# Filling the block-diagonal packed keys of an attention and SwiGLU chain: eight quarter copies and subtractions, or one masked multiplication and a split

## The chip, the cores and the metric

The kernel runs on one core of a Trainium2 chip. The metric is the device time of one execution in microseconds (us), as the median of several executions. TensorE (PE) does the matmuls, VectorE (DVE), ScalarE (ACT) and GpSimd (POOL) the elementwise work, and SyncE (SP) issues most transfers. PEld in the profile is TensorE's weight load.

## The reference, cut to what matters

```python
def sm_attn(qq, kk, vv):
    s = scale * np.matmul(qq, kk.transpose(0, 1, 3, 2))
    s = s - np.max(s, axis=-1, keepdims=True)
    a = np.exp(s)
    a = a / (np.sum(a, axis=-1, keepdims=True) + 1e-09)
    return np.matmul(a, vv)

p_packed = sm_attn(p, k, v)               # 32 packed rows per head
out = sm_attn(q, p_packed, p_packed)      # 576 rows per head, over the 32
x = out rearranged to (4608, 512)
h = x @ w_in; x = (h / (1 + np.exp(-h))) @ w_out
y = (((x @ w1) * (x @ w2)) @ w3) @ w_out2
```

q, k and v are (8, 8, 576, 64): batch, head, row, head dimension. All of it is float32.

## The kernel before, in words

**Precision.** Most float32 products are done as three matmuls (`mm3`, L97): each operand is split into a rounded high part and the low rest (`split`, L93; its copy is recorded as L82 on ScalarE or L86 on VectorE, its subtraction as L91 on VectorE or GpSimd). The three matmuls are recorded as L98, L99 and L100. The first two batches work "plain", with one float32 matmul and no split (L294).

**The main loop** (L1278) runs over 256 items (batch, half of the rows, block of 128 of the 2048 hidden columns). For each item `emit_h` (L826) does six matmuls into `ps_h`, `emit_g` (L839) makes the tanh on ScalarE (`sg`, L841), the product on VectorE (`gg`, L846) and its split into `gh` (ScalarE) and `gl` (GpSimd), and `emit_x2` (L853) does twelve matmuls for the item three places earlier. `ps_h` has two buffers. Weights `mq` of the first product are fetched by `fetch` (L782) and split by VectorE (a cast, L86) and GpSimd (L91). At the end of a half, VectorE and ScalarE move the sums out (`xs`, L883).

**Beside the items** run streams of steps with their own pace (L1087 to L1110): attention for later batches (`Pack` and `Spread`), the weights of the packed rows (`PackIn`), and the decoding of later weights. After item 255 comes a second stage (from L1315), in which nothing of this change runs.

**The part in question.** `Pack` makes the packed rows of four heads at a time (a batch has two such groups, `hg` 0 and 1). After its last product ScalarE scales the result into `pk` (L464), VectorE transposes it into `pkT` (128 x 64: four heads by 32 rows, two halves of the head dimension; L469), and `fill_blocks` (L247, called in L470) writes it into the diagonal blocks of `sbd`, a tile of 128 rows by 2 (high, low) x 2 x 128. The rest of that tile is zero: `blocks` (L221) sets it to zero on GpSimd when it is first made (four tiles, made once plain and once split: eight times). Four quarters of 32 rows are copied one by one, on ScalarE when plain (4 fills) and on VectorE when split (12 fills, batches 2 to 7); when split, four subtractions on VectorE follow for the low parts. `Spread` (L566, L567) later uses `sbd` as the weights of the scores of q (`ps_s`). After the fill, `Pack.tail` (L473) writes the packed rows into `mbd` on VectorE (L490, L492).

**Order of the work.** The instructions of an engine run in the order in which the framework has put them when the program is built, by their place in the program, what they depend on, and a simulated timeline (L1655). The steps of the first 70 us are written out in a list (L70).

`work` (L244) is a pool of three buffers, used for `e1`, `s2` and `sT`.

Of the kernel before, what the change touches and what calls it, by code (L numbers as in the profile page):

```python
# [9 lines left out]
F32 = mybir.dt.float32  # L10
F32R = mybir.dt.float32r
# [4 lines left out]
ALU = mybir.AluOpType  # L16
# [7 lines left out]
def attention_swiglu_chain(  # L24
# [54 lines left out]
    V, A, T, G, DMA = nc.vector, nc.scalar, nc.tensor, nc.gpsimd, nc.sync  # L79
# [4 lines left out]
    def split_hi(hi, src, on_vector=False):  # L84
        if on_vector:
            V.tensor_copy(out=hi, in_=src)  # L86
        else:
            act_copy(hi, src)

    def split_lo(lo, src, hi, eng=None):  # L90
        (eng or V).tensor_tensor(out=lo, in0=src, in1=hi.bitcast(F32), op=ALU.subtract)  # L91

    def split(hi, lo, src, on_vector=False, eng=None):  # L93
        split_hi(hi, src, on_vector)
        split_lo(lo, src, hi, eng)
# [40 lines left out]
    dram = ctx.enter_context(tc.tile_pool(name="dram", bufs=1, space=bass.MemoryType.DRAM))  # L136
    const = ctx.enter_context(tc.tile_pool(name="const", bufs=1))
    ident = const.tile([128, 128], F32, name="ident")

    wi_d = dram.tile([4, DM, 512], F32, name="wi_d")  # L140
    w12_d = dram.tile([128, KM2 // 2, 2, 7, 2, 2, 128], F32, name="w12_d")
# [7 lines left out]
    at = attn.enter_context(tc.tile_pool(name="at", bufs=1, side="right"))  # L149
# [71 lines left out]
    def blocks(name, shape, plain):  # L221

        if zeroed.get(name, (None, None))[0] != plain:
            t = at.tile(shape, F32 if plain else F32R, tag=name, name=name)
            G.memset(t if plain else t.bitcast(F32), 0.0)
            zeroed[name] = plain, t
        return zeroed[name][1]

    def q_blocks(i, plain):
        return blocks(f"sbd{i}", [128, 2, 2, 128], plain)  # L230

    def m_blocks(plain):
        return blocks("mbd", [128, 2, CD, 2, 2, 32], plain)
# [10 lines left out]
    def work(shape, name):  # L244
        return at.tile(shape, F32, tag="work", name=name, bufs=3)

    def fill_blocks(dst, src, plain):  # L247

        quads = [slice(32 * h, 32 * h + 32) for h in range(4)]
        for r in quads:  # L250
            (act_copy if plain else V.tensor_copy)(dst[r, 0, :, r], src[r])
        for r in () if plain else quads:
            V.tensor_tensor(
                out=dst[r, 1, :, r], in0=src[r], in1=dst[r, 0, :, r].bitcast(F32), op=ALU.subtract
            )

    acc = {}

# [100 lines left out]
    class Pack(Rows):  # L359
# [58 lines left out]
        def steps(self):  # L418
# [49 lines left out]
            pkT = at.tile([128, 2, 32], F32, tag="pkT", name="pkT", bufs=2)  # L468
            V.transpose(out=pkT, in_=self.pk[:, 0].rearrange("p (e i) -> p e i", e=2))  # L469
            fill_blocks(q_blocks(2 * (b % 2) + hg, self.lane.plain), pkT, self.lane.plain)  # L470
            yield

# [77 lines left out]
    class Spread(Rows):  # L550
# [11 lines left out]
        def steps(self):  # L562
            b, hg, hv = self.b, self.hg, self.halves
            if b not in a2:
                a2[b] = a2_p.tile([128, 2, 2, S], F32R, tag="a2", name="a2")
            qb = q_blocks(2 * (b % 2) + hg, self.lane.plain)  # L566
            sc = self.scores([qb[:, x] for x in range(2)])  # L567
            n = HB * len(hv)
# [50 lines left out]
        units[-1].tail()  # L619

    make_identity(nc, ident)
    for i in range(2):
        q_blocks(i, True)
    m_blocks(True)

    left = ctx.enter_context(ExitStack())
# [472 lines left out]
    for b in range(2, B - 2, 2):  # L1099
        n, at0 = b + 2, b * H2  # L1100
# [558 lines left out]
```

## Time and profile before

| | us |
|---|---|
| median of 3 executions (1412.35 to 1413.73) | 1413.46 |
| the profiled execution | 1412.14 |
| its span (first to last instruction) | 1410.3 |
| TensorE busy in it | 1362.6 |
| VectorE busy | 1007.0 |
| GpSimd busy | 904.7 |
| ScalarE busy | 732.7 |

The page gives busy time by engine, 40 slices of the span, the chain of work that ended last, and the costliest groups. An instruction's duration in the trace includes time in which it stood blocked after its start, so the same form can be long or short. Idle time before an instruction is put down to what ended it.

### The profile page before, as it was taken

What the parts mean: (1) busy time and instruction counts of PE and PEld (TensorE: products, weight loads), DVE (VectorE), ACT (ScalarE), POOL (GpSimd) and SP (SyncE); (2) the same over time, 40 slices, a digit from 0 to 9 for tenths busy, and PEclk for the clock granted to TensorE, in tenths of its full rate; (3) what the DMA queues carried; (4) which work ended last, traced back from release to release, by engine and by line L of the source; (5) the groups of instructions that cost most, each with busy time, mean ns of one, the idle gap of its engine ahead of it and who ended that gap; (6) DMA issues with size and microseconds to landing.
All of it is one profiled execution on the core that took longest, in us unless ns stands there. A gap on an engine that the chain in (4) does not pass through costs nothing. (4 is left out here: it accounts for less than half of the span.)

```text
span 1410.3 us, 26742 instructions
## 1 busy us (share of the span) xinstructions
PE 1362.6 (97%) x9197; PEld 1313.7 (93%) x9197; DVE 1007.0 (71%) x1760; ACT 732.7 (52%) x1641; POOL 904.7 (64%) x855
## 2 busy tenths in 40 slices
PE   7799899999999999999999999999999999999998
PEld 5488799999899998999999999899999999999998
DVE  5887857668877569887769756776675766656755
ACT  6866555655666565575455644543344343433432
POOL 2778855865779766789577553756574755737632
PEclk9899999999999999999999999999999999999999
DMA  8688544754667535685457648756667676566751
GB/s 311 202 285 284 161 150 136 226 161 135 199 195 223 168 121 143 197 256 155 135 172 242 213 138 280 231 167 207 209 173 218 206 210 209 170 215 206 214 164 53
DMA packets 191558, 272.95 MB, mean 194 GB/s; under 512 B 18752, under 2 KB 112320, under 8 KB 191424
## 3 DMA queue, kind: packets, MB, share of 16 engines
q1 hardware_dynamic: 173168, 251.20, 57.9%
q10 hardware_dynamic: 18256, 20.06, 4.1%
q8 instruction: 73, 1.20, 0.4%
q14 instruction: 61, 0.50, 0.1%
HBM read 209.06 MB, written 62.13 MB: 192 GB/s over the span
## 5 line engine op out<-in xcount | busy, mean ns | idle before, releaser
L98 PE MATMUL ps_x<-gh,wo 128*128 128x288 f32 x1024 | 301.3, 297 | 3.7 <-DVE xs L883 2.4
L99 PE MATMUL ps_x<-gh,wo 128*128 128x288 f32 x1024 | 300.6, 296 | 0.0
L91 POOL TENSOR_TENSOR gl<-gg,gh 128x288 fp32r<-128x288 f32 x256 | 229.5, 899 | 99.3 <-ACT gh L82 77.6
L100 PE MATMUL ps_x<-gl,wo 128*128 128x288 f32 x1024 | 290.3, 297 | 2.0 <-POOL gl L91 1.7
L1481 DVE TENSOR_TENSOR o<-o,ps_o 128x768 f32<-128x768 f32 x137 | 130.1, 952 | 103.3 <-PE ps_o L1499 102.5
L98 PEld LDWEIGHTS ps_x<-gh,wo 128*128 128x128 f32 x1024 | 192.2, 188 | 7.0 <-DVE xs L883 3.2
L91 POOL TENSOR_TENSOR mq<-mr,mq 128x256 fp32r<-128x256 f32 x168 | 140.6, 837 | 90.1 <-DVE mq L86 43.4
L99 PEld LDWEIGHTS ps_x<-gh,wo 128*128 128x128 f32 x1024 | 192.6, 188 | 2.0 <-issue 1.2
L100 PEld LDWEIGHTS ps_x<-gl,wo 128*128 128x128 f32 x1024 | 188.3, 188 | 5.0 <-POOL gl L91 4.1
L846 DVE SCALAR_TENSOR_TENSOR gg<-sg,ps_h 128x288 f32<-128x288 f32 x256 | 114.7, 448 | 107.1 <-ACT sg L841 68.6
L82 ACT ACTIVATE gh<-gg 128x288 fp32r<-128x288 f32 x256 | 112.7, 442 | 149.4 <-DVE gg L846 137.7
L98 PE MATMUL ps_h<-a,mq 128*128 128x288 f32 x512 | 156.2, 305 | 17.6 <-DVE gg L846 13.2
L99 PE MATMUL ps_h<-a,mq 128*128 128x288 f32 x512 | 152.3, 297 | 0.0
L100 PE MATMUL ps_h<-a,mq 128*128 128x288 f32 x512 | 151.9, 297 | 0.0
L91 POOL TENSOR_TENSOR lfa<-y,lfa 128x384 fp32r<-128x384 f32 x69 | 78.7, 1141 | 104.5 <-ACT lfa L82 92.2
L841 ACT ACTIVATE sg<-ps_h 128x288 f32<-128x288 f32 x256 | 103.2, 405 | 79.8 <-PE ps_h L100 50.7
L98 PEld LDWEIGHTS ps_h<-a,mq 128*128 128x128 f32 x512 | 96.8, 189 | 26.6 <-DVE gg L846 19.4
L1499 PE MATMUL ps_o<-w,lfs 128*128 128x256 f32 x828 | 119.3, 282 | 1.9 <-DVE o L1481 1.5
L1341 PE MATMUL ps_a<-xct,ws 128*128 128x384 f32 x576 | 116.3, 335 | 0.4 <-ACT p L82 0.4
L1499 PEld LDWEIGHTS ps_o<-w,lfs 128*128 128x128 f32 x828 | 112.3, 189 | 2.7 <-DVE o L1481 1.8
L1341 PEld LDWEIGHTS ps_a<-xct,ws 128*128 128x128 f32 x576 | 100.1, 188 | 0.7 <-ACT p L82 0.7
L99 PEld LDWEIGHTS ps_h<-a,mq 128*128 128x128 f32 x512 | 96.9, 189 | 2.7 <-issue 1.0
(217 smaller groups left out, 3297.5 us busy)
## 6 DMA issues: line engine op xcount, KB each, us to landing
ws<-w_d SPq DMA_DIRECT2D x192, 256.0 KB, 3.0
wa<-w_d SPq DMA_DIRECT2D x144, 256.0 KB, 3.1
mr<-m_d SPq DMA_DIRECT2D x144, 128.0 KB, 2.5
raw<-in_moe_w_dram SPq DMA_DIRECT2D x32, 512.0 KB, 4.3
w_d<-w12s ACTq DMA_DIRECT2D x56, 256.0 KB, 2.7
wz<-wi_d SPq DMA_DIRECT2D x48, 256.0 KB, 3.9
m_d<-ms SPq DMA_DIRECT2D x96, 128.0 KB, 3.0
x_d<-xs SPq DMA_DIRECT2D x20, 576.0 KB, 3.4
```

The source lines that it names most:

```text
L82: return A.activation(out=dst, in_=src, func=ACTF.Copy, scale=mul)
L91: (eng or V).tensor_tensor(out=lo, in0=src, in1=hi.bitcast(F32), op=ALU.subtract)
L98: T.matmul(out=dst, lhsT=wh, rhs=xh, start=start, stop=False)
L99: T.matmul(out=dst, lhsT=wl, rhs=xh, start=False, stop=False)
L100: return T.matmul(out=dst, lhsT=wh, rhs=xl, start=False, stop=stop)
L841: ins = A.activation(out=sg, in_=ps, func=ACTF.Tanh, scale=0.5)
L846: ins = V.scalar_tensor_tensor(out=gg, in0=sg, scalar=1.0, in1=ps, op0=ALU.add, op1=ALU.mult)
L1341: ins = T.matmul(out=bank, lhsT=w[:, kt, wp], rhs=xt[:, kt, xp], start=first and (kt, n) == (0, 0), stop=last and (kt, n) == (1, 2), skip_ ...
L1481: V.tensor_tensor(out=oacc[k], in0=oacc[k], in1=ps, op=ALU.add)
L1499: T.matmul(out=ps[:, t], lhsT=l[:, lp], rhs=w[:, wp], start=fresh and t != 1 and n == 0, stop=done and t != 0 and n == 2, skip_group_check ...
```

## The change

A constant `mask` of 128 x 4 has a one where row / 32 equals the column. `fill_blocks` multiplies `pkT`, spread over four heads, by the mask, spread over the 32 rows, on VectorE in one instruction that writes the whole 128 x 256 block, zeros included. When plain, it writes `sbd` directly. When split, it writes a `work` buffer, ScalarE copies the high part out of it, and GpSimd subtracts for the low part. The zeroing of `sbd` goes; five small memsets for the mask come at the start. `m_blocks` stays as it was.

```diff
+    mask = const.tile([128, 4], F32, name="mask")
...
+    sbd = {}
+
     def q_blocks(i, plain):
-        return blocks(f"sbd{i}", [128, 2, 2, 128], plain)
+
+        if sbd.get(i, (None, None))[0] != plain:
+            sbd[i] = plain, at.tile([128, 2, 2, 128], F32 if plain else F32R, tag=f"sbd{i}", name=f"sbd{i}")
+        return sbd[i][1]
...
     def fill_blocks(dst, src, plain):
 
-        quads = [slice(32 * h, 32 * h + 32) for h in range(4)]
-        for r in quads:
-            (act_copy if plain else V.tensor_copy)(dst[r, 0, :, r], src[r])
-        for r in () if plain else quads:
-            V.tensor_tensor(
-                out=dst[r, 1, :, r], in0=src[r], in1=dst[r, 0, :, r].bitcast(F32), op=ALU.subtract
-            )
+        wide = [128, 2, 4, 32]
+        whole = dst[:, 0] if plain else work([128, 2, 128], "blk")
+        V.tensor_tensor(
+            out=whole.rearrange("p e (h n) -> p e h n", h=4), in0=src.unsqueeze(2).to_broadcast(wide),
+            in1=mask.unsqueeze(1).unsqueeze(3).to_broadcast(wide), op=ALU.mult,
+        )
+        if not plain:
+            split(dst[:, 0], dst[:, 1], whole, eng=G)
...
-    for i in range(2):
-        q_blocks(i, True)
+    G.memset(mask, 0.0)
+    for h in range(4):
+        G.memset(mask[32 * h:32 * h + 32, h:h + 1], 1.0)
     m_blocks(True)
```

## Rows read from the trace of the kernel before

**Rows 1.** The page, part 1: busy time by engine over the span.

```profile
PE 1362.6 (97%) x9197; PEld 1313.7 (93%) x9197; DVE 1007.0 (71%) x1760; ACT 732.7 (52%) x1641; POOL 904.7 (64%) x855
```

**Rows 2.** Busy time by stretch: us, PE, PEld, DVE, ACT, POOL; clock, DMA share, GB/s.

```profile
30.00:40.00 10.00, 8.58 (x36) 5.57 (x35) 9.90 (x27) 9.91 (x25) 5.33 (x4) 1.00 0.59 190
40.00:50.00 10.00, 8.13 (x30) 4.80 (x28) 7.39 (x17) 9.77 (x25) 5.07 (x5) 1.00 0.65 204
50.00:60.00 10.00, 6.36 (x22) 4.36 (x22) 9.24 (x16) 9.88 (x25) 7.78 (x6) 0.66 0.13 47
...
165.00:170.00 5.00, 2.72 (x21) 2.48 (x20) 4.88 (x7) 0.36 (x2) 5.00 (x6) 0.99 0.41 119
170.00:175.00 5.00, 4.27 (x21) 3.98 (x21) 4.73 (x11) 0.80 (x3) 2.52 (x4) 0.67 0.44 131
```

**Rows 3.** Timeline of DVE in the first split fill: start, us, work [idle before it].

```profile
164.41 2.92 DVE L251 CAST sbd<-pkT 32x64 fp32r<-32x64 f32 x4
167.36 1.82 DVE L86 CAST mq<-mr 128x256 fp32r<-128x256 f32 x1
169.10 0.44 DVE L846 SCALAR_TENSOR_TENSOR gg<-sg,ps_h 128x288 f32<-128x288 f32 x1
169.47 3.63 DVE L253 TENSOR_TENSOR sbd<-pkT,sbd 32x64 fp32r<-32x64 f32 x4
```

**Rows 4.** Timeline of POOL over the same stretch.

```profile
164.30 0.74 POOL L91 TENSOR_TENSOR mq<-mr,mq 128x256 fp32r<-128x256 f32 x1
164.99 1.58 POOL L91 TENSOR_TENSOR gl<-gg,gh 128x288 fp32r<-128x288 f32 x2
166.52 0.75 POOL L91 TENSOR_TENSOR mq<-mr,mq 128x256 fp32r<-128x256 f32 x1
167.21 3.10 POOL L91 TENSOR_TENSOR v<-vr,v 128x768 fp32r<-128x768 f32 x2
```

**Rows 5.** Timeline of PE at split fills: the instructions before which it sat idle.

```profile
169.60 0.40 PE L98 MATMUL ps_h<-a,mq 128*128 128x288 f32 x1 [2.28 <-DVE gg L846]
...
174.25 0.38 PE L98 MATMUL ps_s<-x,pb 128*128 128x288 f32 x1 [0.73 <-DVE mbd L492]
...
379.51 0.40 PE L98 MATMUL ps_x<-gh,wo 128*128 128x288 f32 x1 [2.20 <-DVE xs L883]
...
530.36 0.40 PE L98 MATMUL ps_h<-a,mq 128*128 128x288 f32 x1 [0.70 <-DVE gg L846]
...
532.67 0.40 PE L98 MATMUL ps_s<-x,sbd 128*128 128x288 f32 x1 [0.85 <-DVE s L571]
...
575.45 0.40 PE L98 MATMUL ps_h<-a,mq 128*128 128x288 f32 x1 [0.98 <-DVE gg L846]
```

**Rows 6.** Groups of instructions by form, the fills: count | busy us, mean ns | idle before.

```profile
L251 DVE CAST sbd<-pkT 32x64 fp32r<-32x64 f32 x48 | 22.7, 473 | 1.2
...
L253 DVE TENSOR_TENSOR sbd<-pkT,sbd 32x64 fp32r<-32x64 f32 x48 | 19.3, 402 | 1.3
...
L82 ACT ACTIVATE sbd<-pkT 32x64 f32<-32x64 f32 x16 | 4.0, 251 | 0.5 <-DVE pkT L469 0.3
...
L225 POOL MEMSET sbd<- 128x512 f32 x8 | 4.1, 526 | 3.4 <-PE ps_s L294 2.4 <-ACT e L82 1.0
```

**Rows 7.** Groups by form, the nearest work of the new instructions' kinds and sizes.

```profile
L965 DVE TENSOR_TENSOR sums<-z,sums 128x256 f32<-128x256 f32 x8 | 3.5, 442 | 0.0
...
L91 DVE TENSOR_TENSOR pb<-pr,pb 128x256 fp32r<-128x256 f32 x12 | 8.3, 688 | 0.0
...
L576 DVE TENSOR_TENSOR s<-s,mx 128x288 f32<-128x288 f32 x4 | 1.8, 446 | 0.0
...
L82 ACT ACTIVATE pb<-pr 128x256 fp32r<-128x256 f32 x12 | 4.8, 402 | 0.0
...
L91 POOL TENSOR_TENSOR mq<-mr,mq 128x256 fp32r<-128x256 f32 x168 | 140.6, 837 | 90.1 <-DVE mq L86 43.4 <-issue 12.0 <-PE ps_x L100 7.8
```

**Rows 8.** Instructions on the tile sbd: count, ns min/median/max, first and last start.

```profile
L251 DVE CAST sbd<-pkT x48: 174/310/1772, 164.4 to 592.8; 32x64 fp32r<-32x64 f32 x48
...
L98 PE MATMUL ps_s<-x,sbd x48: 288/295/407, 233.2 to 685.8; 128*128 128x288 f32 x48
```

**Rows 9.** Timeline of the plain fills of the second batch, and PE's wait between them.

```profile
40.16 0.51 ACT L82 ACTIVATE sbd<-pkT 32x64 f32<-32x64 f32 x2
...
41.10 0.52 ACT L82 ACTIVATE sbd<-pkT 32x64 f32<-32x64 f32 x2
...
52.35 1.03 ACT L82 ACTIVATE sbd<-pkT 32x64 f32<-32x64 f32 x4
...
53.02 0.58 PE L98 MATMUL ps_h<-a,mq 128*128 128x288 f32 x1 [3.97 <-DVE mq L91]
```

**Rows 10.** Who waited for whom, all of the span: total us, times, longest.

```profile
PE ps_h L98 <- DVE gg L846: 13.2, 14, 3.1
...
PE ps_x L100 <- POOL gl L91: 1.7, 3, 1.2
```

## The prediction

> **What bounds the kernel now.** I read the busy times first. TensorE is busy for 1362.6 of 1410.3 us and VectorE for 71% [rows 1]: VectorE's time is worth nothing as such, and the change can win only what TensorE stands idle (47.7 us in all) or loses in clock. So I looked for the places where a fill makes TensorE idle, in the stretches and then in the timelines.
>
> In the first split fill (164 to 173 us) the reader sees it happen. Four casts of 32 x 64 take 2.92 us and the four subtractions 3.63 us [rows 3], though the shortest cast takes 174 ns [rows 8]. Meanwhile GpSimd runs one instruction after another [rows 4]: the four casts end about where its four instructions from 164.30 to 167.27 us end, one each. An instruction with its operands in SBUF on VectorE evidently waits here for the running GpSimd instruction, so eight small instructions cost eight such waits. `gg` waits behind them until 169.10 us [rows 3], and TensorE, which needs the bank that `gg` frees, idles 2.28 us, then 0.73 us behind `mbd`, queued after the subtractions [rows 5]. In the same stretch the granted clock falls to a mean of 0.67, right after the idle time [rows 2].
>
> Four of the twelve split fills show such idle time. Rows 5 hold all six waits next to fills: 2.28 + 0.73 + 2.20 + 0.70 + 0.85 + 0.98 = 7.74 us. The other eight show none worth counting.
>
> **The change part by part.**
>
> *VectorE in split fills.* Removed are 48 casts (22.7 us) and 48 subtractions (19.3 us), 42.0 us of queue time [rows 6], or 3.5 us a fill. Added are 12 multiplications over 128 x 256. The trace has no multiplication by a mask; the same size with two SBUF operands takes 442 ns little disturbed and 688 ns on average [rows 7], and a broadcast operand costs nothing visible (446 ns for 288 columns, `s<-s,mx` [rows 7]). I take 0.69 us, 8.3 us in all. From below it is 12 x 0.44 = 5.3 us, from above one wait for half of the split of `v` (3.10 / 2 = 1.55 us [rows 4]) in each fill: 12 x 1.99 = 23.9 us. So 18 to 37 us of queue time go, some 34 at the value taken. It pays where it stood ahead of `gg`, `xs`, `mbd` and `s`, which is the 7.74 us; elsewhere VectorE's saving is hidden by TensorE's work.
>
> *ScalarE in split fills.* 12 copies at 402 ns [rows 7], 4.8 us. ScalarE is busy 0.36 of 5 us in the first fill [rows 2], so the copy lies in idle time. It waits for the multiplication, and `gh` and `sg` stand behind it, but `gh` waited there for `gg` anyway. Cost nothing; with that cover gone, 0.40 us a fill.
>
> *GpSimd in split fills.* 12 subtractions at 837 ns [rows 7], 10.0 us. GpSimd is full in the first fill (5.00 of 5 us [rows 2]), and `gl` stands in its queue; TensorE uses `gl` three items later and has waited for it 1.7 us in the whole span [rows 10]. Such a subtraction also makes a VectorE instruction wait once. From below the cost is 0, from above all twelve, 10.0 us. I take the four fills at which TensorE shows no slack now: 4 x 0.84 = 3.4 us. As a check on this value: the Trainium skill says (SBUF — State Buffer, Who interferes with whom) that a VectorE instruction with two SBUF inputs, or in a two-port mode, and a GpSimd instruction that reads SBUF exclude each other for the whole instruction. The first fill agrees (eight waits for eight instructions). By that rule alone the subtraction on GpSimd would be charged in all twelve fills, 10.0 us, and the sum below would be 0.4 us instead of 7.0; that is the first of the rivals.
>
> *The split fill's result.* Its chain becomes longer by two engines, but `sbd` is first read at 233.2 us, 69 us after the first fill began [rows 8]. Nobody waits for it.
>
> *Clock.* A mean of 0.67 over 5 us [rows 2], with 1.2 and 2.4 GHz as its levels, is 5 x 0.33 = 1.65 us lost. If the idle time before it goes, this comes back; from below 0.
>
> *Plain fills.* 16 copies on ScalarE, 4.0 us [rows 6], become 4 multiplications on VectorE, 1.8 us at 0.44. From 30 to 60 us ScalarE is the fullest engine, 29.6 of 30 us, with VectorE at 26.5 [rows 2]. Of the two fills there, one (1.03 us) lies before TensorE's wait of 3.97 us at 53.02 and one just after the work that ends it [rows 9]. I take 1.0 us for the first. From above it is both, 2.06 us; from below a loss of two multiplications on VectorE, 0.9 us.
>
> *The rest.* Eight memsets of 526 ns leave GpSimd, with 2.4 us of waits for TensorE before them [rows 6]; five small ones come at the start. Nothing on the path waits for them now, so 0; if GpSimd were the bound there, a gain up to 4.1 us less five short memsets. The multiplication's buffer is a fourth user of the three `work` buffers: its older users are done by then, so 0, and one wait of the size seen, up to 2.28 us, if not. No transfer is added or moved on any queue, SP's and GpSimd's included.
>
> *Sum.* 7.74 + 1.65 + 1.0 - 3.4 = 7.0 us. The profiled execution took 1412.14 us (its span and 1.8 us around it), 1.3 us under the median of 1413.46. So 1405.1 us for an execution like it, and **1406.4 us** for the median. What is late next in the first fill is the `mq` cast (1.82 us [rows 3]), still ahead of the next `gg`.
>
> **The rivals.**
>
> *Given back on VectorE (0.18).* The waits at fills go, but others on VectorE take their place: the added GpSimd subtraction makes one VectorE instruction wait in every fill (12 x 0.84 = 10.0 us, a gain of 0.4, 1413.1), or the next late thing ahead of `gg` is an `mq` cast that GpSimd blocks, and only the start's 1.0 us is left (1412.5). For it: the one-for-one pattern of the first fill [rows 3, 4], and TensorE's waits for `gg`, 13.2 us in all [rows 10], of which only 2.28 + 0.70 + 0.98 are at fills. Against it: each fill loses eight small instructions that can wait and gets one that can and one that makes others wait. The rule of the Trainium skill cited above is this mechanism.
>
> *GpSimd in front of `gl`, slower (0.12).* Each subtraction goes ahead of `gl` on a full GpSimd, and TensorE waits for it each time: 12 x 0.84 = 10.0 us, with the waits for `gg` replaced and not removed: 1413.46 + 10.0 = 1423.5, or about 1418 if half of the fills pay. It decides once more is paid than won: with 7.74 + 1.65 us back it needs over eleven fills, with nothing back over three (0.2%, 2.8 us). Against it: the 1.7 us in all that TensorE waits for `gl` [rows 10], and three items of slack.
>
> *More than counted (0.10).* The shorter queue also spares TensorE waits that lie some microseconds after fills, of the 13.2 us [rows 10]. With half of the 9.2 us that are not in rows 5, and no loss at GpSimd: 1406.4 - 4.6 - 3.4 = 1398.4; anything under 1402 counts here.
>
> *The change doing something else.* The framework puts the order of every engine's work together anew. I hold that to one wait more or fewer of the size seen, about 2 us, which the range takes in.
>
> **How the numbers follow.** The forecast, about 1402 to 1410.6, has 0.60. A measurement of this kernel can tell about 0.2%, 2.8 us, from no change: faster is under 1410.6, slower over 1416.3. Faster is the forecast and "more", 0.70; no change is the case given back, 0.18; slower is the GpSimd case, 0.12. The range goes down to the case of all waits returned with no new ones (7.74 + 1.65 + 2.06 = 11.4, 1402.0; with a little of "more", 1401.5) and up to nothing won, 1413.5. Outside lie the slower case and most of "more", 0.20 together.
>
> **What would show it.** Right: around 164 to 175 us VectorE has one multiplication of 0.4 to 2 us in the place of 6.5 us, `gg` follows within 2 us, TensorE's six waits at the fills are gone, and the clock near 170 us is 1.00. TensorE's busy time falls by about the clock's part only, its idle time by about 5 us. The GpSimd case shows as TensorE waiting for `gl`, the case given back as the same idle time put down to other `gg`. The forecast is wrong if the waits at the fills are gone and the span is not shorter, or if they stay although VectorE's queue is shorter.

## The result and the profile after

The changed kernel takes 1401.92 us (median of 6 runs, 1399.62 to 1404.67), the kernel before, on the same chip, 1413.6 us (6 runs, 1412.17 to 1414.73). The ratio is 0.9919 with a 95% interval of 0.9905 to 0.9934: about 11.5 us faster. The prediction said 1406.4 with a range from 1401.5 to 1413.5, so the result lies at the lower end of the range, just under the border of 1402 at which the rival "more than counted" began. One of the five executions of `plain_vector_copies` below (1883.41 us, at a mean granted clock of 0.654) was a slow one and is left out of its ratio.

The profiled execution of the changed kernel is the fastest of its six, 1399.62 us with a span of 1397.8 us. Its page, part 1, answers to [rows 1]:

```profile
PE 1353.8 (97%) x9197; PEld 1309.6 (94%) x9197; DVE 984.5 (70%) x1680; ACT 732.2 (52%) x1637; POOL 909.9 (65%) x864
```

VectorE lost 22.5 us and 80 instructions, GpSimd gained 5.2 us. TensorE's busy time fell by 8.8 us, its idle time from 47.7 to 44.0 us, by 3.7.

The first split fill is what the change was read from. The timeline of VectorE in the changed kernel there (start, us, work), answering to [rows 3]:

```profile
163.66 0.50 DVE L257 TENSOR_TENSOR blk<-pkT,mask 128x256 f32<-128x256 f32 x1
164.09 0.81 DVE L854 SCALAR_TENSOR_TENSOR gg<-sg,ps_h 128x288 f32<-128x288 f32 x2
164.87 0.22 DVE L497 CAST mbd<-ps_pk 64x64 fp32r<-64x64 f32 x1
165.01 0.68 DVE L86 CAST mq<-mr 128x256 fp32r<-128x256 f32 x1
```

One multiplication of 0.50 us stands in the place of 6.55 us of casts and subtractions, and `gg` begins 0.43 us after its start. The `mq` cast behind it takes 0.68 us where it took 1.82. TensorE's stretches, answering to [rows 2] (us, PE, PEld, DVE, ACT, POOL; clock, DMA share, GB/s), show no idle time and the full clock, where there were 2.72 and 4.27 of 5 us and clocks of 0.99 and 0.67:

```profile
165.00:170.00 5.00, 5.00 (x40) 5.00 (x39) 2.40 (x8) 1.21 (x4) 4.73 (x6) 1.00 0.47 106
170.00:175.00 5.00, 5.00 (x41) 5.00 (x40) 4.43 (x13) 4.14 (x13) 1.18 (x2) 1.00 0.54 131
```

But a slow stretch of the clock of the same size stands elsewhere in the changed kernel. It lies before the first split fill, where the kernel before has 1.00, and follows a wait of TensorE for `gg`:

```profile
151.96 0.41 PE L98 MATMUL ps_h<-a,mq 128*128 128x288 f32 x1 [3.26 <-DVE gg L854]
```

The stretches there:

```profile
150.00:155.00 5.00, 3.04 (x15) 2.99 (x16) 3.77 (x10) 3.42 (x11) 3.95 (x5) 0.76 0.84 205
155.00:160.00 5.00, 5.00 (x38) 5.00 (x37) 3.02 (x7) 2.26 (x6) 5.00 (x7) 0.90 0.92 288
```

It loses 5 x 0.24 + 5 x 0.10 = 1.7 us, as much as the prediction's 1.65.

Over the other split fills the six waits of [rows 5] are gone, and three others stand next to fills. The timeline of TensorE in the changed kernel, the instructions with their waits:

```profile
377.32 0.40 PE L98 MATMUL ps_h<-a,mq 128*128 128x288 f32 x1 [0.46 <-DVE gg L854]
...
394.04 0.40 PE L98 MATMUL ps_s<-x,sbd 128*128 128x288 f32 x1 [0.21 <-DVE s L578]
...
522.96 0.37 PE L98 MATMUL ps_s<-x,sbd 128*128 128x288 f32 x1 [2.92 <-DVE mbd L499]
```

That is 3.59 us in place of 7.74. Away from the fills waits have gone and come as well: counted from the traces, all of TensorE's waits over 0.15 us between 160 and 650 us fell from 11.4 us (13 waits) to 7.2 (10). The last one above is new, and its cause is on VectorE, read from two timelines of the changed kernel. First VectorE:

```profile
514.56 0.45 DVE L257 TENSOR_TENSOR blk<-pkT,mask 128x256 f32<-128x256 f32 x1
514.93 1.94 DVE L86 CAST mq<-mr 128x256 fp32r<-128x256 f32 x1
...
518.79 3.14 DVE L91 TENSOR_TENSOR w12s<-z,w12s 128x256 fp32r<-128x256 f32 x1
521.85 0.20 DVE L497 CAST mbd<-ps_pk 64x64 fp32r<-64x64 f32 x1
```

Then GpSimd over the same stretch:

```profile
518.68 0.85 POOL L91 TENSOR_TENSOR gl<-gg,gh 128x288 fp32r<-128x288 f32 x1
519.49 0.73 POOL L91 TENSOR_TENSOR mq<-mr,mq 128x256 fp32r<-128x256 f32 x1
520.18 0.72 POOL L91 TENSOR_TENSOR sbd<-blk,sbd 128x256 fp32r<-128x256 f32 x1
520.86 0.79 POOL L91 TENSOR_TENSOR gl<-gg,gh 128x288 fp32r<-128x288 f32 x1
```

The subtraction of `w12s` takes 3.14 us, the longest of twenty (shortest 0.41, median 0.51). It ends 0.28 us after the fourth of the GpSimd instructions that ran without a gap since it began; the third of them is the subtraction that the change added. `mbd` stands behind it, and TensorE behind `mbd`.

The new instructions, in the changed kernel's groups by form (count | busy us, mean ns | idle before):

```profile
L91 POOL TENSOR_TENSOR sbd<-blk,sbd 128x256 fp32r<-128x256 f32 x12 | 9.6, 800 | 0.8 <-ACT sbd L82 0.8
...
L257 DVE TENSOR_TENSOR blk<-pkT,mask 128x256 f32<-128x256 f32 x12 | 7.4, 617 | 0.1
...
L82 ACT ACTIVATE sbd<-blk 128x256 fp32r<-128x256 f32 x12 | 5.0, 415 | 1.6 <-DVE blk L257 0.8
L257 DVE TENSOR_TENSOR sbd<-pkT,mask 128x256 f32<-128x256 f32 x4 | 3.6, 897 | 0.1
```

So the prices were near those taken (0.69, 0.84 and 0.40 us in split fills); only the four plain multiplications cost 0.90 us and not 0.44.

What the prediction does not explain is the start. Before the first split fill the changed kernel is already ahead: the first `gg` begins at 51.4 us where it began at 54.3, the 25th at 134.2 where it was 139.4. The stretch from 0 to 100 us in the windows of the changed kernel:

```profile
0.00:100.00 100.00, 81.96 (x404) 64.20 (x405) 83.25 (x159) 68.97 (x158) 59.13 (x59) 0.97 0.83 279
```

The kernel before has here:

```profile
0.00:100.00 100.00, 80.25 (x361) 60.87 (x362) 73.94 (x148) 72.04 (x171) 56.76 (x57) 0.91 0.78 262
```

VectorE is 9.3 us busier, ScalarE 3.1 us less, and TensorE has issued 43 matmuls more. The prediction had put 1.0 us there. The long wait beside which it counted that, 3.97 us at 53.02 [rows 9], has not gone: one of nearly the same length stands in its place, and ends with a copy on ScalarE.

```profile
49.81 0.90 PE L679 MATMUL ps_m<-zi,mbd 128*128 128x512 f32 x1 [3.54 <-ACT mbd L82]
```

### The profile page after: what moved, and what is told of

The parts are those of the page before. It is cut to its first block, busy times and chain, and to the rows that moved or that the text cites. A ratio compares the mean times of both kernels' runs of the same rounds, so it can differ in the third digit from the quotient of the medians.

```text
span 1397.8 us, 26672 instructions
## 1 busy us (share of the span) xinstructions
PE 1353.8 (97%) x9197; PEld 1309.6 (94%) x9197; DVE 984.5 (70%) x1680; ACT 732.2 (52%) x1637; POOL 909.9 (65%) x864
## 5 line engine op out<-in xcount | busy, mean ns | idle before, releaser
L98 PE MATMUL ps_h<-a,mq 128*128 128x288 f32 x512 | 156.0, 305 | 10.9 <-DVE gg L854 10.8
L98 PEld LDWEIGHTS ps_h<-a,mq 128*128 128x128 f32 x512 | 97.1, 190 | 16.4 <-DVE gg L854 13.4
L86 DVE CAST mq<-mr 128x256 fp32r<-128x256 f32 x168 | 94.6, 564 | 21.3 <-DMA mr<-m_d 19.1
```

The source lines that it names most:

```text
L98: T.matmul(out=dst, lhsT=wh, rhs=xh, start=start, stop=False)
```

## The experiments

All ratios are against the kernel before, on the same chip, with their 95% intervals; one thousandth is 1.4 us, and differences between kernels are taken from the ratios. The interval of one ratio reaches some 2 us to either side. The difference of two ratios is therefore uncertain by some 2.8 us (an estimate: the root of the sum of the two squared half-widths).

The traces also tell which runs kept the order of work. In `neutral_mask` TensorE, VectorE and ScalarE run all their instructions in the order of the kernel before; in `split_only` they do so up to the first split fill, but for one matmul. `sub_on_vector` and `four_multiplications` keep the changed kernel's order up to there. Every run that touches the plain work of the start has another order. Of TensorE's first 750 to 770 instructions (to 165 us), 188 to 347 stand elsewhere than in the kernel that the run is to be compared with, when the two sequences are compared without the instructions that the edit adds or takes away.

**One part at a time.** `plain_only` has the multiplication in plain fills alone; split fills go by quarters into zeroed blocks, as before:

```diff
     def q_blocks(i, plain):
 
+        if not plain:
+            return blocks(f"sbd{i}", [128, 2, 2, 128], plain)
...
     def fill_blocks(dst, src, plain):
 
+        if not plain:
+            quads = [slice(32 * h, 32 * h + 32) for h in range(4)]
+            for r in quads:
+                (act_copy if plain else V.tensor_copy)(dst[r, 0, :, r], src[r])
+            for r in () if plain else quads:
+                V.tensor_tensor(
+                    out=dst[r, 1, :, r], in0=src[r], in1=dst[r, 0, :, r].bitcast(F32), op=ALU.subtract
+                )
+            return
         wide = [128, 2, 4, 32]
```

> Only the four plain fills are made by the masked multiplication; the twelve split fills stay as eight small instructions, with their zeroing. Theory A (ScalarE's queue is the path of the first 60 us, so every plain fill returns its 1.03 us): 4 to 5 us under the kernel before, ratio about 0.9968, and ScalarE 3 to 4.5 us further at item 0. Theory B (the start gives the 1.0 us of the prediction, and the rest of the 11.7 us is at the split fills): 1 us, ratio 0.9993. Theory C (the gain is mostly a lucky new order of the queues): anything, not adding up with the split part alone to 11.7 us.

Measured: 0.9965 [0.9955, 0.9975], 1408.81 us beside 1413.97, 5.0 us faster, with an interval from 3.5 to 6.4 us.

`split_only` is the other half; plain fills go by four ScalarE copies into zeroed blocks, as before:

```diff
     def q_blocks(i, plain):
 
+        if plain:
+            return blocks(f"sbd{i}", [128, 2, 2, 128], plain)
...
     def fill_blocks(dst, src, plain):
 
+        if plain:
+            quads = [slice(32 * h, 32 * h + 32) for h in range(4)]
+            for r in quads:
+                (act_copy if plain else V.tensor_copy)(dst[r, 0, :, r], src[r])
...
+            return
         wide = [128, 2, 4, 32]
```

> Only the twelve split fills are changed; the four plain ones stay as ScalarE copies. Theory A: about 7 us under the kernel before (ratio 0.995), the six waits at fills gone. Theory B: about 10 to 11 us (0.9925). Theory C: does not add up with the plain part alone.

Measured: 0.9957 [0.9944, 0.9969], 1406.65 us, 6.1 us faster by the ratio (0.0043 x 1413.6). The two ratios multiply to 0.9922, against 0.9919 for the whole change: the parts add up, and each is worth about half. As the order of work up to the first split fill is that of the kernel before, what this run wins there comes from the fill and not from a new order. Its profiled execution is 1408.25 us, 1.6 over its median and only 3.9 under that of the kernel before, so its trace shows less than the 6.1 us.

**A mask that nobody reads.** `neutral_mask` tells whether the new tile and memsets move the time by themselves.

```diff
+mask = const.tile([128, 4], F32, name="mask")
+G.memset(mask, 0.0)
+for h in range(4):
+    G.memset(mask[32 * h:32 * h + 32, h:h + 1], 1.0)
```

> The kernel before with the mask and its five memsets, which nothing reads: work of no use and 0.5 us on GpSimd at the start. Theories A and B: no change, within 1 us of the kernel before. Theory C (a new order of the queues alone moves the time): a change of several us, either way.

Measured: 0.9994 [0.9985, 1.0003], 1412.89 us: no change. The order of work did not change either, so this run says nothing on theory C.

**Where the low part is subtracted.** `sub_on_vector` is the changed kernel with the subtraction on VectorE.

```diff
-split(dst[:, 0], dst[:, 1], whole, eng=G)
+split(dst[:, 0], dst[:, 1], whole)
```

> The changed kernel with the subtraction for the low part on VectorE in place of GpSimd in the twelve split fills. Theory A (GpSimd's subtraction costs the path nothing, VectorE's queue ahead of gg is what counts): equal to the changed kernel or up to 3 us slower, as VectorE gets 12 x 0.7 = 8 us more. Theory D, the prediction's term (the subtraction on GpSimd costs the path 3.4 us): up to 3 us faster than the changed kernel.

Measured: 0.9922 [0.9909, 0.9936], 1402.56 us, as the changed kernel. VectorE's two groups by form in this kernel:

```profile
L257 DVE TENSOR_TENSOR blk<-pkT,mask 128x256 f32<-128x256 f32 x12 | 10.1, 839 | 0.1
...
L91 DVE TENSOR_TENSOR sbd<-blk,sbd 128x256 fp32r<-128x256 f32 x12 | 7.6, 632 | 1.8 <-ACT sbd L82 1.7
```

VectorE has 10.3 us more to do in the fills (17.7 against 7.4), and the time is the same within the intervals. Putting the subtraction on GpSimd thus costs no more than putting it on VectorE, whose queue has room for it. The wait of 2.92 us has shrunk to 0.78, and others have come; TensorE's timeline in this kernel next to fills:

```profile
170.93 0.37 PE L98 MATMUL ps_s<-x,pb 128*128 128x288 f32 x1 [0.95 <-DVE mbd L499]
...
374.79 0.37 PE L98 MATMUL ps_s<-x,pb 128*128 128x288 f32 x1 [0.54 <-DVE mbd L499]
...
525.29 0.37 PE L98 MATMUL ps_s<-x,sbd 128*128 128x288 f32 x1 [0.78 <-DVE mbd L499]
```

**ScalarE's time at the start.** `idle_scalar_copies` gives ScalarE back its four copies of each plain fill, into a buffer that nobody reads.

```diff
     ...
+    if plain:
+        spare = at.tile([128, 64], F32, tag="spare", name="spare")
+        for h in range(4):
+            r = slice(32 * h, 32 * h + 32)
+            act_copy(spare[r].rearrange("p (e n) -> p e n", e=2), src[r])
     if not plain:
         split(dst[:, 0], dst[:, 1], whole, eng=G)
```

> The changed kernel, and beside each of the four plain multiplications ScalarE again makes the four quarter copies, into a buffer that nobody reads. Only ScalarE's queue time of the plain fills comes back, 4 x 1.03 us; multiplication, order and the gone zeroing stay. Theory A (the start's gain is ScalarE's queue time): 4 to 5 us slower than the changed kernel, about as fast as with the split fills alone changed (ratio 0.995 to 0.996 to the kernel before). Theory E (the start's gain is the gone zeroing on GpSimd or an earlier result for TensorE): as fast as the changed kernel, ratio 0.992.

Measured: 0.9931 [0.9918, 0.9945], 1403.6 us. The groups by form show that the load was there, as in [rows 6]:

```profile
L82 ACT ACTIVATE spare<-pkT 32x64 f32<-32x64 f32 x16 | 4.0, 250 | 0.5 <-DVE pkT L481 0.3
```

Only some 1.7 us of the 5 come back, less than expected and less than the 2.8 us that two ratios can tell apart: ScalarE's queue time by itself does not account for the 5 us. The expectation that the order stays did not hold (225 of TensorE's first 772 instructions stand elsewhere), so the run does not give back ScalarE's time alone.

**Plain fills by four VectorE copies.** `plain_vector_copies` takes the work off ScalarE without the mask.

```diff
...
     def fill_blocks(dst, src, plain):
 
+        if plain:
+            quads = [slice(32 * h, 32 * h + 32) for h in range(4)]
+            for r in quads:
+                V.tensor_copy(dst[r, 0, :, r], src[r])
...
+            return
```

> The changed kernel, with the four plain fills made by four quarter copies on VectorE into zeroed blocks, in place of the multiplication. ScalarE is relieved just as much. Theory A: within 1.5 us of the changed kernel (ratio 0.991 to 0.993). Theory E (the gone zeroing counts): 2 us or more slower than it.

Measured: 0.9934 [0.9921, 0.9948], 1403.65 us. That is 2.1 us slower than the changed kernel, just past theory E's mark and again under 2.8 us, so it decides between neither. Some 3 of the start's 5 us are there without the multiplication and with the zeroing.

**The multiplication in four pieces.** `four_multiplications` cuts the split fill's multiplication by heads (`parts` is four slices of one head there, and one of all four in plain fills), so VectorE does the same columns in four times the instructions.

```diff
+for hs in parts:
+    wide = [128, 2, hs.stop - hs.start, 32]
     V.tensor_tensor(
-        out=whole.rearrange("p e (h n) -> p e h n", h=4), in0=src.unsqueeze(2).to_broadcast(wide),
-        in1=mask.unsqueeze(1).unsqueeze(3).to_broadcast(wide), op=ALU.mult,
+        out=whole.rearrange("p e (h n) -> p e h n", h=4)[:, :, hs], in0=src.unsqueeze(2).to_broadcast(wide),
+        in1=mask[:, hs].unsqueeze(1).unsqueeze(3).to_broadcast(wide), op=ALU.mult,
     )
```

> The changed kernel with each split fill's multiplication cut into four, one a head, 128 x 64 each: the same elements in four instructions. Theory F (an instruction with SBUF operands waits for a running GpSimd instruction, so the number of instructions is what a fill costs): the four take 0.35 to 0.5 us each on average where one alone would take about 0.2, VectorE is 8 to 15 us busier than in the changed kernel, and the time is 0 to 3 us longer. Rival G (the quarters were slow because 32 x 64 pieces are slow as such): each takes 0.2 to 0.25 us, VectorE 2 to 4 us busier, no change in the time.

Measured: 0.9924 [0.9911, 0.9937], 1402.22 us, as the changed kernel. Its group by form:

```profile
L259 DVE TENSOR_TENSOR blk<-pkT,mask 128x64 f32<-128x64 f32 x48 | 19.6, 467 | 0.0
```

A piece takes 210 ns at the least but 467 on average: queue time of the fills rose from 7.4 to 19.6 us by the number of instructions. Counted from the trace, the 16 pieces that ran while GpSimd had no instruction took 214 ns on average, the other 32 took 594. Rival G is ruled out: small pieces are fast unless GpSimd runs. That is the mechanism by which the eight small instructions cost 3.5 us a fill. But 12.2 us of queue time, given back in this form, did not lengthen the time by anything measurable. What queue time costs depends on where it lies: before, 6.55 us stood in one fill around the `gg` that TensorE waited for. That this place is what made the fill cost time is read from the trace; no run put as much queue time back at this place alone.

**The plain multiplication on GpSimd.** `plain_on_gpsimd`:

```diff
-V.tensor_tensor(
+(G if plain else V).tensor_tensor(
```

> The changed kernel with the four plain multiplications on GpSimd, which from 30 to 50 us has room where ScalarE and VectorE are full. Theory A: ScalarE is relieved as before and VectorE by 4 x 0.4 to 1.2 us more, at 0.75 to 0.9 us on GpSimd: 0 to 2 us faster than the changed kernel (ratio 0.9905 to 0.992). If the fill's result is on the path there, up to 1.5 us slower.

Measured: 0.9923 [0.9909, 0.9936], 1401.68 us, as the changed kernel. VectorE's 3.6 us for these four at the start made no difference that the runs can tell.

**The result by way of ScalarE.** `plain_via_scalar` multiplies on VectorE into a work buffer, and ScalarE copies it into the block: readers wait for ScalarE's queue again, but with one copy for four.

```diff
-whole = dst[:, 0] if plain else work([128, 2, 128], "blk")
+whole = work([128, 2, 128], "blk")
...
+if plain:
+    act_copy(dst[:, 0], whole)
```

> The changed kernel, but in the four plain fills the multiplication writes a work buffer and ScalarE copies it into the block: 0.42 us of ScalarE a fill (1.7 us in all, against 4.1 before), and the block is again ready only when ScalarE's queue comes to it. Theory H (the rest of the start's 5 us is that TensorE and what follows no longer wait for ScalarE's queue to come to the fill): 2.5 to 4 us slower than the changed kernel, ratio 0.994 to 0.995. Theory A2 (only ScalarE's queue time counts, at the 1.5 us that the idle copies of 4.1 us cost): 0.6 us slower, ratio 0.992 to 0.9925.

Measured: 0.9930 [0.9918, 0.9943], 1402.67 us, about 1.6 us slower than the changed kernel by the ratios, between the two theories and under 2.8 us.

**A multiplication that nobody reads.** `idle_multiplication` is `split_only` with the plain multiplication beside ScalarE's copies.

```diff
...
+        if plain:
+            quads = [slice(32 * h, 32 * h + 32) for h in range(4)]
+            for r in quads:
+                (act_copy if plain else V.tensor_copy)(dst[r, 0, :, r], src[r])
+            V.tensor_tensor(
+                out=work([128, 2, 128], "blk").rearrange("p e (h n) -> p e h n", h=4),
+                in0=src.unsqueeze(2).to_broadcast([128, 2, 4, 32]),
+                in1=mask.unsqueeze(1).unsqueeze(3).to_broadcast([128, 2, 4, 32]), op=ALU.mult,
+            )
...
+            return
```

> The split fills changed, the plain fills by ScalarE's copies as before, and beside them the masked multiplication into a buffer that nobody reads. The order of the queues is made anew, the block still comes from ScalarE. Theory H: as the split fills alone, or up to 1 us slower, ratio 0.9955 to 0.9965. Theory C for the start (a new order there gains by itself): 2 us or more faster than the split fills alone, ratio under 0.9945.

Measured: 0.9946 [0.9928, 0.9963], 1404.69 us. It does more work than `split_only` and is, if anything, some 1.6 us faster; the intervals overlap, and its order of work is another (330 of TensorE's first 752 instructions), so it decides nothing but that the multiplication showed no cost.

**The next copies off ScalarE.** `mbd_on_vector` moves the plain copies of `mbd` to VectorE too, since ScalarE looked like the queue to relieve.

```diff
-(act_copy if self.place is None else V.tensor_copy)(dst[0], src)
+V.tensor_copy(dst[0], src)
```

> The changed kernel with the plain copies of the packed rows into mbd on VectorE in place of ScalarE (8 of 0.21 us, out of PSUM). In the changed kernel TensorE waits 3.5 us once for such a copy, which stands in ScalarE's queue. Theory H: the same step once more, 1 to 3 us faster than the changed kernel, ratio 0.990 to 0.9915. Against it: VectorE is as full there as ScalarE (9.92 of 10 us from 40 to 50), then no change.

Measured: 0.9944 [0.9930, 0.9957], 1405.5 us, about 3.5 us slower than the changed kernel. Relieving ScalarE further did not pay here. VectorE was already busy for 83 of the first 100 us, and the order of work is another; the run does not tell which of the two costs.

**Both loads on ScalarE.** `idle_and_via_scalar` puts the unread copies and the copy into the block together on ScalarE, in that order.

```diff
     ...
+    if plain:
+        spare = at.tile([128, 64], F32, tag="spare", name="spare")
+        for h in range(4):
+            r = slice(32 * h, 32 * h + 32)
+            act_copy(spare[r].rearrange("p (e n) -> p e n", e=2), src[r])
+        act_copy(dst[:, 0], whole)
```

> The changed kernel; in the four plain fills ScalarE makes the four idle quarter copies and after them copies the product into the block: 5.8 us of ScalarE in all, and the block comes at the end of it, as in the kernel before and a little later. Theory A3 (ScalarE's time and the late result each cost, and together they are the start's gain): as slow as with the split fills alone changed, ratio 0.995 to 0.9965. Theory C for the start (the gain there is the order of the queues that goes with the multiplication, worth 2 to 4 us): it stays at the ratio of either alone, 0.993.

Measured: 0.9940 [0.9926, 0.9955], 1405.69 us, 3.0 us slower than the changed kernel, just over what two ratios can tell apart and about the sum of the two single effects. With `split_only` at 0.9957 some 2 us of the start's 5 are still without an owner.

When the work arrives shows where each kernel gains. The starts of `gg` in each profiled execution, in us (n counts from 1; counted from the traces):

```
kernel                 n=1     25     31     34     75    110    256
before                54.3  139.4  159.7  174.6  301.4  410.4  862.8
neutral_mask          54.0  138.2  158.5  173.7  301.8  411.1  863.2
plain_only            52.7  132.1  153.9  167.6  298.9  407.5  859.8
split_only            54.3  138.8  159.2  168.9  301.7  406.1  858.3
idle_scalar_copies    55.2  135.8  158.1  166.9  297.2  402.3  855.2
plain_via_scalar      51.3  135.0  156.1  163.4  296.9  401.5  853.0
idle_and_via_scalar   53.9  136.8  158.7  167.1  300.4  405.2  858.0
sub_on_vector         53.8  136.7  159.2  167.0  297.8  402.9  853.3
four_multiplications  52.4  135.9  159.1  168.7  296.1  403.6  851.7
changed kernel        51.4  134.2  157.4  164.5  295.3  399.8  850.8
```

The changed kernel, `sub_on_vector` and `four_multiplications` have the same order of work up to n=31, and the same work but for the split fills: that their first `gg` lie 2.4 us apart is not the edits' doing, and no single start can be read more finely than that.

The stretch from n=31 to 34 holds the first split fill. It takes 14.9 us before, 15.2 with the unread mask, 9.7 in `split_only` and 7.1 in the changed kernel. The start's lead at n=25 is 5.2 us in the changed kernel and 7.3 in `plain_only`, and shrinks to 2.3 and 5.8 by n=31 (0.5 and 0.6 in `sub_on_vector` and `four_multiplications`, where 3.6 and 5.3 us stand at n=75). `gg` counts the items alone, while TensorE also works for the streams beside them, so a lead in `gg` need not last: in `split_only` the 5.7 us at n=34 are gone at n=75, and 4.3 us are there at n=110, past the fill at which the wait of 2.20 us for `xs` [rows 5] is gone. From n=256 on nothing more is won, as the 12.0 us there are the difference of the spans (12.5) but for 0.5.

## Why the prediction was right or wrong

**Right: the first split fill, in mechanism.** The step said that small VectorE instructions wait for GpSimd, that `gg` and TensorE stand behind them, and that one multiplication ends it. The first fill shows each part, and `split_only` shows it in the old order of work. The count was too high: six of the eight instructions waited, not eight. The first subtraction took 2.37 us, through several GpSimd instructions, the second 0.73 us; the last two together took 0.47 us, after GpSimd's run had ended at 172.52 us. The timelines of GpSimd and VectorE in the kernel before, the last of each:

```profile
171.72 0.80 POOL L91 TENSOR_TENSOR gl<-gg,gh 128x288 fp32r<-128x288 f32 x1
```

```profile
172.63 0.47 DVE L253 TENSOR_TENSOR sbd<-pkT,sbd 32x64 fp32r<-32x64 f32 x2
```

**Right in sum by luck, not in its terms: the split fills' 7.74 + 1.65 - 3.4 = 6.0 us.** `split_only` measures 6.1, but none of the three terms came out as priced.

- *Six waits of TensorE gone, 7.74 us.* They are gone, but the waits at fills went to 3.59 us, not to zero, and other waits came in between: from 160 to 650 us TensorE's waits over 0.15 us fell by 4.2 us in the changed kernel and by 3.4 (11.4 to 8.0) in `split_only`. The wait of 2.92 us is the rival "given back on VectorE" happening once in twelve fills; one of 2.94 us in front of matmuls of the same kind, behind `mbd`, is in `split_only` as well (at 529.22 us), and one of 1.13 us in `four_multiplications`.
- *The clock, 1.65 us.* Near 170 us it is 1.00, as said, but the same loss stands elsewhere: 1.7 us between 150 and 160 us in the changed kernel. In `split_only` the granted clock is 0.66 from 155 to 160 us and 0.50 from 530 to 535, after the wait of 2.94 us. So no run shows the term as won.
- *GpSimd, -3.4 us.* With the subtraction on VectorE (`sub_on_vector`) other waits stand at the fills and the time is the same within the intervals. So no run shows a price of the subtraction on GpSimd.

**Wrong: the plain fills, "I take 1.0 us for the first".** They are worth about 5.0 us (`plain_only`, 3.5 to 6.4), more than the bound from above (2.06 us) allowed. That is 4.0 of the 4.5 us by which 1406.4 missed. The step took the copies' own time in front of one wait of TensorE, and of two of the four fills at most. That wait stayed nearly as long (3.54 for 3.97 us), so the gain is not there. The prediction had read that ScalarE was full from 30 to 60 us and had foreseen a new order of every engine's work, but held it to about 2 us either way.

What makes the 5 us is not shown. ScalarE's queue time (1.7 us, `idle_scalar_copies`) and the way of the result through ScalarE's queue (1.6 us, `plain_via_scalar`) are candidates, together 3.0 (`idle_and_via_scalar`); each by itself is smaller than two ratios can tell apart, and some 2 us have no candidate among them. The new order of the queues is the rival for all of it: each of these runs has an order of its own, and `neutral_mask`, which was to test the order, kept the old one. Against it as a simple cause stands only `plain_on_gpsimd`, where 188 of TensorE's first 772 instructions stand elsewhere and the time is that of the changed kernel.

**Wrong: where it would show in TensorE's times.** I said that busy time falls by the clock's part only and idle time by about 5 us. Busy time fell by 8.8, idle time by 3.7. Part of this is clock: from 0 to 200 us the granted clock's shortfall is 100 x 0.09 + 40 x 0.04 = 10.6 us before and 100 x 0.03 + 60 x 0.03 = 4.8 after (windows of 0 to 100, 100 to 160, 160 to 200 us). But that shortfall is not time on the path: `neutral_mask` has 100 x 0.05 + 60 x 0.03 = 6.8 us of it and takes as long as the kernel before, and `idle_and_via_scalar` grants 1.00 over the first 100 us and is slower than the changed kernel. While TensorE waits for other engines anyway, a slower matmul only turns idle time into busy time.

**The rivals.** "GpSimd in front of `gl`, slower" did not occur: TensorE waits for `gl` 0.2 us in the changed kernel, once (1.7 us in [rows 10]). "More than counted" came true in its number (1401.92, under 1402), by another way: the waits for `gg` fell only from 13.2 to 10.8 us, and the surplus is of the size that `plain_only` wins over the 1.0 us taken.

**Costs taken as nothing.** The ScalarE copy (5.0 us in all), the memsets (`neutral_mask`) and the longer way to the split result showed no cost; the first split `sbd` is filled at 163.7 us and first read by TensorE at 228.2.

**The Trainium skill's rule.** By the Trainium skill's rule of exclusion (SBUF — State Buffer, Who interferes with whom) the sum would have been 0.4 us instead of 7.0, an estimate. The runs measure 11.5. The trace of the kernel before agrees with the rule for the single instructions: the 48 subtractions of the split fills, with two inputs in SBUF, took 660 ns on average when GpSimd ran something and 217 when it ran nothing. But whether TensorE has to wait for a blocked instruction is another question, and charging each one was wrong here.

## What to carry to other kernels

In this kernel many small VectorE instructions with their operands in SBUF cost a wait each while GpSimd was busy; one wide instruction that does more arithmetic was cheaper in queue time, and gained where TensorE waited behind that queue. A stall that is removed can come back elsewhere: add up all waits, and the clock, over a longer stretch before calling a term won.

Look at the engine that is full for tens of microseconds at the start, even if it is half idle over the span: taking the four fills off it, with the new order of work that came along, was worth about as much as the stall that the eye is drawn to. Check such a reading by giving the load back unread. Then compare the order of work in the traces: a control whose order did not change cannot clear a new order, and a run whose order did change does not isolate the load.

## What the runs showed of the hardware

A VectorE instruction that waits for GpSimd can wait through several GpSimd instructions, not one. The subtraction of `w12s` above waited through four (3.14 us, against 0.41 at the least), and it need not be a large one: in `split_only` a 128 x 1 operation takes 2.14 us, as VectorE's timeline shows,

```profile
173.01 2.14 DVE L442 TENSOR_TENSOR nb<-mx 128x1 f32<-128x1 f32 x1
```

and ends where GpSimd's instructions do that follow each other without a gap:

```profile
172.88 0.73 POOL L91 TENSOR_TENSOR mq<-mr,mq 128x256 fp32r<-128x256 f32 x1
173.57 1.56 POOL L91 TENSOR_TENSOR gl<-gg,gh 128x288 fp32r<-128x288 f32 x2
```

So the prediction's price from above, one wait for half of the split of `v` in each fill, is no bound on what a single instruction can wait. Whether an instruction waits goes with where its operands lie: in the kernel before, counted from its trace, the 96 instructions of the split fills took 204 ns on average when GpSimd ran nothing and 670 ns when it ran something (48 of each), while the casts and subtractions of `mbd`, which read PSUM, took 216 and 222 ns.
